# Two groups' weight gradients kept on chip until the last head, and stored in row pieces

## The chip, the cores and the metric

The kernel runs on one core of one Trainium2 chip. The time is what the device takes for one execution, in microseconds, as a median of several runs. A profile of one execution shows the engines (PE for matrix products, DVE, ACT and POOL for the rest, SP for issuing transfers) and the 16 DMA engines that carry every transfer between the device's memory and the chip.

## The reference

The program is the backward pass of one decode step: attention with 32 heads over a cache of 8192 keys and values, beside a gated MLP, both fed by one normalised row. It returns the forward output and the gradients of everything but the MLP's own input.

```python
def _A_ref(x, k_cache, v_cache, wq, wo):          # x: 1 x 1 x 640, caches: 1 x 32 x 8192 x 128
    q = (x @ wq).reshape(B, Sq, Hq, Dh)...
    scores = jnp.einsum("bhqd,bhkd->bhqk", q, k) * (Dh ** -0.5)
    p = _softmax(scores, axis=-1)
    o = jnp.einsum("bhqk,bhkd->bhqd", p, v)
    return o...reshape(B, Sq, Hq * Dh) @ wo

def _B_ref(x, w1, w3, w2):                        # 640 -> 1728 -> 640
    return (silu(x @ w1) * (x @ w3)) @ w2

xn = _layernorm(x)
out = x + _A_ref(xn, ...) + _B_ref(xn, ...)

_out, _vjp = jax.vjp(_f, A_x, A_k_cache, A_v_cache, A_wq, A_wo, B_w1, B_w3, B_w2)
return (out, *_vjp(grad_out))
```

The gradients of the two caches are as large as the caches, 2 MB per head each in bf16. Those of `wq` and `wo` are outer products with one row, 5 MB each in all.

## The kernel before

Head by head, the K and V tiles (128 partitions of 16 KB) are loaded into one of ten slots (`free_slots`, `load_next`), used, overwritten in place with their gradients (`outer`, L474, on DVE) and stored from the same slot (`store`, L485). Loads (L111) and stores (L106) are all issued by SP, in the order in which the program calls them: `store` of a tile is followed by `load_next`, which takes the oldest free slot, and so has to wait until that slot's own store has landed.

Heads come in eight groups of four (`NG`, `GH`), each with a slice of `wq` (`wq_g`, 128 x 5 x 512) and of `wo` (`wo_g`, 128 x 4 x 640), 640 KB each. They live in a pool of three buffers. In the heads after a group has ended, its slices are overwritten with their gradients: `fin_wo` (L521) in the first head of the next group, `fin_wq` (L527), one of five columns `ci` at a time, in the second and third (`side_k`, `side_m`, `side_v`). POOL issues the stores: wo in one transfer (L515), wq a column at a time (L535). After the last column the buffers are free, and POOL loads the slices of the group three ahead (L119, L121); the last such load is that of group 7, after group 4.

The last group's gradients, after head 31, leave in rows: 68 on SP, then 5 and 55 on POOL (`store_group`):

```python
        fifo(dst[0:68], t[0:68])
        for lo, hi in ((68, 73), (73, P)):
            nc.gpsimd.dma_start(dst[lo:hi], t[lo:hi])
```

After the loop over heads come `outers_a` and `outers_b` of head 31 (its V and K gradients and their stores), then `fin_od`, `fin_pe`, `fin_wo` and five times `fin_wq` for group 7, then the two small outputs.

Of the kernel before, what the change touches and what calls it, by code (L numbers as in the profile page):

```python
# [16 lines left out]
P = 128  # L17
# [4 lines left out]
def kernel(  # L22
# [22 lines left out]
    nc = tc.nc  # L45
    H = A_k_cache.shape[1]
# [8 lines left out]
    NG = H // GH  # L55
# [49 lines left out]
    def fifo(out_, in_):  # L105
        nc.sync.dma_start(out_, in_)  # L106
# [10 lines left out]
    def load_group(g, eng):  # L117
        wq_g = wpool.tile([P, NC, GW], BF16, name="wq_g", tag="wq_g")
        eng.dma_start(wq_g[:], wq_v[:, :, g * GW:(g + 1) * GW])  # L119
        wo_g = wpool.tile([P, GH, D], BF16, name="wo_g", tag="wo_g")  # L120
        eng.dma_start(wo_g[:], wo_v[:, g * GH:(g + 1) * GH, :])  # L121
        grp[g] = dict(wq=wq_g, wo=wo_g)
# [175 lines left out]
    hd = {}  # L298
# [180 lines left out]
    def outer_v(h, lo, hi):  # L479
        outer(kv_tiles[("V", h)], hd[h]["qd"][:, 1, :], hd[h]["P2"], lo, hi)  # L480

    def outer_k(h, lo, hi):
        outer(kv_tiles[("K", h)], hd[h]["qd"][:, 0, :], hd[h]["U2"], lo, hi)

    def store(kind, h):  # L485
        t = kv_tiles.pop((kind, h))
        if kind == "K":
            hd.pop(h)
        fifo((dkc if kind == "K" else dvc)[h], t[:])
        free_slots.append(t)  # L490
        load_next()
# [18 lines left out]
        for hh in range(GH):  # L510
            out_row(G_["od_bf"][:, hh, 0:1], G_["wo"][:, hh, :])

    def store_group(g, dst, t):
        if g < NG - 1:
            nc.gpsimd.dma_start(dst, t[:])  # L515
            return
        fifo(dst[0:68], t[0:68])
        for lo, hi in ((68, 73), (73, P)):
            nc.gpsimd.dma_start(dst[lo:hi], t[lo:hi])

    def fin_wo(g):  # L521
        G_ = grp[g]
        for hh in range(GH):
            nc.vector.tensor_scalar(G_["wo"][:, hh, :], g_bc[:], G_["od"][:, hh, 0:1], None, ALU.mult)
        store_group(g, dwo_v[:, g * GH:(g + 1) * GH, :], G_["wo"])

    def fin_wq(g, ci):  # L527
        G_ = grp[g]
        wq_g, dqb = G_["wq"], G_["dqb"]
        nc.vector.scalar_tensor_tensor(wq_g[:, ci, :], wq_g[:, ci, :], 1.0, dqb, ALU.mult, ALU.mult,  # L530
                                       accum_out=dxa[:, ci, g:g + 1])
        nc.vector.tensor_scalar(wq_g[:, ci, :], dqb, xn_col[:, ci:ci + 1], None, ALU.mult)  # L532
        dwq_g = dwq_v[:, :, g * GW:(g + 1) * GW]
        if g < NG - 1:
            nc.gpsimd.dma_start(dwq_g[:, ci, :], wq_g[:, ci, :])  # L535
        if ci == NC - 1:
            if g == NG - 1:
                store_group(g, dwq_g, wq_g)
            grp.pop(g)
            if g + 3 < NG:  # L540
                load_group(g + 3, nc.gpsimd)
# [147 lines left out]
    gate = consts.tile([P, 1], F32, name="gate")  # L689

    def side_k(h):
        g, hh = divmod(h, GH)
        if hh == 1 and g > 0:
            fin_wq(g - 1, 0)
        elif hh == 2 and g > 0:
            fin_wq(g - 1, 3)
        elif hh == 3 and g + 1 < NG:
            prep_do(g + 1, 1)

    def side_m(h):  # L700
        g, hh = divmod(h, GH)
        if hh == 0 and g > 0:
            fin_od(g - 1)
        elif hh == 1 and g > 0:
            fin_wq(g - 1, 1)
        elif hh == 2 and g > 0:
            fin_wq(g - 1, 4)
        elif hh == 3 and g + 1 < NG:
            prep_do(g + 1, 2)
            prep_do(g + 1, 3)  # L710

    def side_v(h):
        g, hh = divmod(h, GH)
        if hh == 0 and g > 0:
            fin_wo(g - 1)
        elif hh == 1 and g > 0:
            fin_wq(g - 1, 2)
        elif hh == 2 and g + 1 < NG:
            prep_new(g + 1)
            prep_do(g + 1, 0)  # L720
        elif hh == 3 and g + 1 < NG:
            prep_cm(g + 1, hd[h]["m"][:, 324:324 + 4 * GH])
# [18 lines left out]
    def outers_a(h):  # L741
        outer_v(h, 0, J // 2)
        outer_v(h, J // 2, J)
        store("V", h)
        outer_k(h, 0, J // 2)

    def outers_b(h):
        outer_k(h, J // 2, J)
        store("K", h)
# [3 lines left out]
    def head(h):  # L753
        nxt = h + 1 < H
        pre = nxt and h + 1 != MLP_AT
        has_prev = h > 0 and h != MLP_AT
        had = (4 if h else 2) if h != MLP_AT else 0
        if nxt:
            new_head(h + 1)
        if has_prev:  # L760
            outers_a(h - 1)
        side_k(h)
        for c in range(had, NCH, 2):
            T(h, "K", c)
            T(h, "K", c + 1)
            if c >= 2:
                Mp(h, "K", c - 2)
            if h > 0 and h % GH == 0 and c == 4:
                col(h - 1)
        T(h, "V", 0)  # L770
        T(h, "V", 1)
        Mp(h, "K", NCH - 2)
        ev(h, "K")
        T(h, "V", 2)
        T(h, "V", 3)
        selm(h, "K")
        mx(h)
        Mp(h, "V", 0)
        T(h, "V", 4)
        mx_bc(h)  # L780
        side_m(h)
        T(h, "V", 5)
        Mp(h, "V", 2)
        expo(h)
        T(h, "V", 6)
        zsum(h)
        probs(h)
        if has_prev:
            outers_b(h - 1)
        side_pe1(h)  # L790
        T(h, "V", 7)
        side_pe1b(h)
        Mp(h, "V", 4)
        side_pe2(h)
        side_v(h)
        if nxt:
            fill_qz(h + 1)
            rows_pe(h + 1, pst()[:, 0:2 * DH], True)
            rows_act(h + 1)
        if pre:  # L800
            T(h + 1, "K", 0)
            T(h + 1, "K", 1)
        Mp(h, "V", NCH - 2)
        ev(h, "V")
        o_sum(h)
        selm(h, "V")
        rdot(h)
        if pre:
            T(h + 1, "K", 2)
        dsum(h)  # L810
        if pre:
            T(h + 1, "K", 3)
            Mp(h + 1, "K", 0)
        dq_sum(h)
        if not nxt:
            col(h)
# [15 lines left out]
    for h in range(H):  # L832
        if h == MLP_AT:
            outers_a(h - 1)
            outers_b(h - 1)
            mlp()
        head(h)
        if h < 2:
            nc.gpsimd.tensor_copy(gate[:], hd[h]["rdot"][:])
            load_group(h + 1, nc.gpsimd)  # L840
    outers_a(H - 1)
    outers_b(H - 1)
    fin_od(NG - 1)
    fin_pe(NG - 1)
    fin_wo(NG - 1)
    for ci in range(NC):
        fin_wq(NG - 1, ci)
# [58 lines left out]
```

## Time and profile before

| what | value |
|---|---|
| median of 3 runs | 730.87 us (730.68 to 731.32) |
| the profiled execution | 730.97 us, of which the span of the profile is 729.2 us |
| busy: PE, DVE, ACT, POOL | 604.1, 459.5, 376.3, 44.0 us |
| bytes moved | 303.53 MB, 416 GB/s over the span |
| queue of SP / of POOL | 277.09 MB / 25.61 MB |

The page gives busy times of the engines, then the span in 40 slices of 18.2 us with the mean busy share of the 16 DMA engines. Further views answer who waited for whom, what ran when, and how busy the engines were in any stretch.

### The profile page before, as it was taken

What the parts mean: (1) busy time and instruction counts of PE and PEld (TensorE: products, weight loads), DVE (VectorE), ACT (ScalarE), POOL (GpSimd) and SP (SyncE); (2) the same over time, 40 slices, a digit from 0 to 9 for tenths busy, and PEclk for the clock granted to TensorE, in tenths of its full rate; (3) what the DMA queues carried; (4) which work ended last, traced back from release to release, by engine and by line L of the source; (5) the groups of instructions that cost most, each with busy time, mean ns of one, the idle gap of its engine ahead of it and who ended that gap; (6) DMA issues with size and microseconds to landing.
All of it is one profiled execution on the core that took longest, in us unless ns stands there. A gap on an engine that the chain in (4) does not pass through costs nothing.

```text
span 729.2 us, 12963 instructions
## 1 busy us (share of the span) xinstructions
PE 604.1 (83%) x5186; PEld 376.4 (52%) x5193; DVE 459.5 (63%) x811; ACT 376.3 (52%) x727; POOL 44.0 (6%) x75
## 2 busy tenths in 40 slices
PE   4989489999899899877886998988898889969930
PEld 2547366665565555544554554554555546545510
DVE  4179646678868776667556665646746657566482
ACT  3640736665665656544554554645554446645510
POOL 0010100010001000101000000000000000000000
PEclk9996799999999999989999998989999989998975
DMA  8999999999999999999999999999999999999994
GB/s 356 394 418 413 432 439 409 418 436 413 422 427 424 425 431 426 428 424 432 420 430 429 431 423 427 426 432 431 422 430 425 433 428 430 431 423 423 429 408 151
DMA packets 24219, 303.53 MB, mean 416 GB/s; under 512 B 3380, under 2 KB 5356, under 8 KB 11487
## 3 DMA queue, kind: packets, MB, share of 16 engines
q1 hardware_dynamic: 17994, 277.09, 89.6%
q0 software_dynamic: 6160, 25.61, 8.8%
q8 instruction: 41, 0.67, 0.4%
q14 instruction: 20, 0.16, 0.1%
q10 hardware_dynamic: 4, 0.00, 0.0%
HBM read 151.34 MB, written 151.34 MB: 415 GB/s over the span
## 4 chain that ended last, share of the span: by engine, by line
DMA 54%; PE 35%; DVE 5%; ACT 2%; issue 1%; SPq 0%; ACTq 0%; DVEq 0%
DMA out_dram<-kv 21%; DMA kv<-in_A_k_cache_dram 18%; PE pT L326 18%; DMA kv<-in_A_v_cache_dram 14%; PE sA L347 5%; PE dA L347 4%; PE X L441 4%; DVE kv L474 3%; PE m L364 2%; DMA wo_g<-in_A_wo_dram 2%; ACT KT L328 1%; PE pT L274 1%; PE m L408 0%; DVE side L265 0%; DVE wq_g L530 0%
## 5 line engine op out<-in xcount | busy, mean ns | idle before, releaser
L328 ACT COPY KT<-pT 128x512 f32<-128x512 f32 x512 | 287.9, 587 | 230.3 <-PE pT L326 210.5
L326 PE MATMUL pT<-ident_f,kv 128*128 128x128 f32 x2048 | 305.9, 288 | 58.6 <-DMA kv<-in_A_k_cache_dram 40.9
L326 PEld LDWEIGHTS pT<-ident_f,kv 128*128 128x128 f32 x2048 | 235.2, 148 | 150.8 <-PE pT L326 53.4
L474 DVE TENSOR_TENSOR kv<-qd,U 128x4096 bf16<-128x4096 bf16 x64 | 146.1, 2285 | 0.0
L474 DVE TENSOR_TENSOR kv<-qd,P 128x4096 bf16<-128x4096 bf16 x64 | 143.6, 2285 | 0.0
L441 PE MATMUL X<-kv,Z 128*32 128x512 bf16 x1024 | 100.3, 424 | 1.8 <-DVE Z L458 1.8
L347 PE MATMUL dA<-KT,qz 128*32 128x512 bf16 x512 | 85.4, 413 | 0.0
L347 PE MATMUL sA<-KT,qz 128*32 128x512 bf16 x512 | 82.6, 402 | 0.0
L424 DVE SCALAR_TENSOR_TENSOR U<-m,P 128x64 bf16<-128x64 f32 x32 | 7.5, 234 | 103.9 <-PE m L364 103.9
L441 PEld LDWEIGHTS <-Z 128*32 128x32 bf16 x1024 | 34.1, 103 | 36.8 <-issue 11.6
L347 PEld LDWEIGHTS <-qz 128*32 128x32 bf16 x1024 | 29.6, 95 | 40.7 <-issue 38.1
L390 DVE TENSOR_REDUCE mrow<-m 128x1 f32<-128x64 f32 x32 | 7.2, 223 | 54.4 <-PE m L364 54.3
L364 PEld LDWEIGHTS m<-selc,KT 64*128 64x128 f32 x256 | 22.2, 148 | 30.4 <-ACT KT L354 17.8
L364 PE MATMUL m<-selc,KT 64*128 64x64 f32 x256 | 31.2, 247 | 7.2 <-ACT KT L354 7.2
L535 POOL DMA_DIRECT2D out_dram<-wq_g x35 | 19.1, 544 | 225.6 <-DVE wq_g L532 130.4
L384 ACT CAST qd<-pT 128x256 bf16<-128x256 f32 x32 | 11.9, 372 | 39.4 <-DVE kv L474 30.4
L397 DVE TENSOR_REDUCE negM<-m 128x1 f32<-128x128 f32 x32 | 9.3, 292 | 33.2 <-PE m L394 33.2
L530 DVE SCALAR_TENSOR_TENSOR wq_g<-wq_g,side 128x512 bf16<-128x512 bf16 x40 | 27.4, 684 | 0.0
L265 DVE SCALAR_TENSOR_TENSOR side<-wo_g,g_bc 128x640 bf16<-128x640 bf16 x32 | 26.3, 820 | 1.1 <-DMA wo_g<-in_A_wo_dram 0.8
L515 POOL DMA_DIRECT2D out_dram<-wo_g x7 | 5.3, 760 | 274.6 <-DVE qz L371 234.5
L456 DVE SCALAR_TENSOR_TENSOR U<-m,P 128x128 bf16<-128x128 f32 x32 | 11.4, 355 | 15.9 <-PE m L454 15.9
L354 ACT COPY KT<-dA 64x512 f32<-64x512 f32 x32 | 18.6, 581 | 4.7 <-PE dA L347 4.6
(163 smaller groups left out, 383.5 us busy)
## 6 DMA issues: line engine op xcount, KB each, us to landing
out_dram<-kv SPq DMA_DIRECT2D x64, 2048.0 KB, 30.8
kv<-in_A_k_cache_dram SPq DMA_DIRECT2D x32, 2048.0 KB, 15.4
kv<-in_A_v_cache_dram SPq DMA_DIRECT2D x32, 2048.0 KB
wq_g<-in_A_wq_dram POOLq DMA_DIRECT2D x7, 640.0 KB, 15.1
wo_g<-in_A_wo_dram POOLq DMA_DIRECT2D x7, 640.0 KB, 22.1
out_dram<-wo_g POOLq DMA_DIRECT2D x7, 640.0 KB, 13.5
out_dram<-wq_g POOLq DMA_DIRECT2D x35, 128.0 KB, 8.2
kv<-in_B_w_dram SPq DMA_DIRECT2D x2, 1728.0 KB
```

What stands on the lines that cost most here:

```text
L265: nc.vector.scalar_tensor_tensor(junk[:], G_["wo"][:, hh, :], 1.0, g_bc[:], ALU.mult, ALU.mult, accum_out=G_["do"][:, hh:hh + 1])
L326: nc.tensor.transpose(pT[:, k * P:(k + 1) * P], W3[:, 4 * c + k, :], ident_f[:])
L328: nc.scalar.copy(KT[:].rearrange("p k w -> p (k w)"), pT[:])
L347: nc.tensor.matmul(S_[kind][q:q + QW, :], lhsT=S_["qz"][:, o:o + QW], rhs=KTb[c][:, par, :], start=(c0 == 0 and par == 0), stop=(c0 == NCH ...
L354: nc.scalar.copy(XS[0:QH].rearrange("p k w -> p (k w)"), S_.pop(kind)[0:QH, :])
L364: nc.tensor.matmul(S_["m"][:, b0:b0 + 4 * J].rearrange("p (x c k t) -> p k x c t", x=4, k=4, t=2)[:, k], lhsT=XS[0:QH, k, :], rhs=selc[0:Q ...
L384: nc.scalar.copy(qd[:].rearrange("p a d -> p (a d)"), hd[h].pop("ps_r"))
L441: nc.tensor.matmul(xg["X"][q:q + QW, :], lhsT=Z[:, o:o + QW], rhs=W[:, N4 * i:N4 * (i + 1)], start=(slot == 0 and i < 4), stop=(slot == NS ...
L456: nc.vector.scalar_tensor_tensor(S_["U2"][:], S_["V"][:, 0:J].unsqueeze(2).to_broadcast([P, J, 2]), S_["m"][:, OC + NS:OC + NS + 1], S_["P ...
L474: nc.vector.tensor_tensor(dst[:, lo * DH:hi * DH].rearrange("p (j a b) -> p j a b", a=DH // 2, b=2), vec.rearrange("p (a b) -> p a b", b=2 ...
L530: nc.vector.scalar_tensor_tensor(wq_g[:, ci, :], wq_g[:, ci, :], 1.0, dqb, ALU.mult, ALU.mult, accum_out=dxa[:, ci, g:g + 1])
L535: nc.gpsimd.dma_start(dwq_g[:, ci, :], wq_g[:, ci, :])
```

## The change

Groups 5 and 6 (`HOLD`) no longer store their gradients when they are ready: `store_group` notes destination and tile in `held`. Four such tiles are collected, wo and wq of group 5, then wo and wq of group 6. wq of these groups also gives up its five columns and is stored whole.

After the loop over heads, before head 31's outer products, POOL copies a value of head 31 (`rdot`) to a scratch tile, so that it waits for it, and `flush(2)` twice sends wo and wq of group 5: 5 and 121 rows on POOL and 2 rows on SP. When wo of group 7 has been sent as before, `flush(68)` sends wo of group 6 as 68 rows on SP and 5 and 55 on POOL, and `flush(2)` its wq as 5, 121 and 2 rows. wq of group 7 is last. On SP the two 2-row pieces of group 5 stand between the store of head 30's K gradient and that of head 31's V gradient.

```diff
+    HOLD = (NG - 3, NG - 2)
+    held = []
+
+    def store_group(g, dst, t, late=(68, 5)):
+        if g in HOLD:
+            held.append((dst, t))
+            return
         if g < NG - 1:
             nc.gpsimd.dma_start(dst, t[:])
             return
-        fifo(dst[0:68], t[0:68])
-        for lo, hi in ((68, 73), (73, P)):
-            nc.gpsimd.dma_start(dst[lo:hi], t[lo:hi])
+        store_rows(dst, t, *late)
+
+    def store_rows(dst, t, n, k):
+        if n < P // 2:
+            cuts = ((0, k), (k, P - n), (P - n, P))
+            hw = 2
+        else:
+            cuts = ((0, n), (n, n + k), (n + k, P))
+            hw = 0
+        for i, (lo, hi) in enumerate(cuts):
+            (nc.sync if i == hw else nc.gpsimd).dma_start(dst[lo:hi], t[lo:hi])
...
         store_group(g, dwo_v[:, g * GH:(g + 1) * GH, :], G_["wo"])
+        if g == NG - 1:
+            flush(68)
+            flush(2)
+
+    def flush(n):
+        dst, t = held.pop(0)
+        store_rows(dst, t, n, 5)
...
-        if g < NG - 1:
+        if g < NG - 3:
             nc.gpsimd.dma_start(dwq_g[:, ci, :], wq_g[:, ci, :])
         if ci == NC - 1:
-            if g == NG - 1:
+            if g >= NG - 3:
                 store_group(g, dwq_g, wq_g)
...
+    nc.gpsimd.tensor_copy(gate[:], hd[H - 1]["rdot"][:])
+    flush(2)
+    flush(2)
     outers_a(H - 1)
     outers_b(H - 1)
     fin_od(NG - 1)
```

More of the change, by code (lines that the diff above doesn't have):

```diff
@@ L511, in fin_pe @@
             out_row(G_["od_bf"][:, hh, 0:1], G_["wo"][:, hh, :])
-    def store_group(g, dst, t):
+    HOLD = (NG - 3, NG - 2)
[4 more added lines that the diff above has]
+            return
         if g < NG - 1:
```

## The prediction, made before the changed kernel was run

> **What bounds the kernel now.** I read the 40 slices of the page first, then SP's waits, then the end of the timeline, then a table of the last 40 us.
>
> ```profile
> DMA  8999999999999999999999999999999999999994
> GB/s 356 394 418 413 432 439 409 418 436 413 422 427 424 425 431 426 428 424 432 420 430 429 431 423 427 426 432 431 422 430 425 433 428 430 431 423 423 429 408 151
> DMA packets 24219, 303.53 MB, mean 416 GB/s; under 512 B 3380, under 2 KB 5356, under 8 KB 11487
> ...
> SPq L111 <- DMA out_dram<-kv: 472.5, 52, 22.4
> SPq L106 <- DVE kv L474: 86.8, 14, 10.5
> ```
>
> The DMA engines are full from the second slice to the last but one. SP, which issues the cache loads (L111), spends 472.5 us in waits until an older cache store has landed and its slot is free. A store has landed when all 16 DMA engines have done their share, so the slowest of them sets the pace. The end shows it:
>
> ```profile
> core 0: us, PE busy (x) PEld busy (x) DVE busy (x) ACT busy (x) POOL busy (x), PEclk, DMA share, GB/s
> ...
> 700.00:705.00 5.00, 0.00 (x0) 0.00 (x0) 5.00 (x3) 0.00 (x0) 0.00 (x0) 0.62 0.95 400
> ...
> 713.00:716.00 3.00, 0.82 (x3) 0.58 (x3) 1.71 (x11) 0.00 (x0) 1.32 (x2) 0.50 0.83 316
> ...
> 718.00:720.00 2.00, 0.00 (x0) 0.00 (x0) 0.00 (x0) 0.00 (x0) 0.00 (x0) 0.50 0.49 147
> ...
> 722.00:724.00 2.00, 0.00 (x0) 0.00 (x0) 0.00 (x0) 0.00 (x0) 0.00 (x0) 0.50 0.08 33
> 724.00:726.00 2.00, 0.00 (x0) 0.00 (x0) 0.00 (x0) 0.00 (x0) 0.00 (x0) 0.50 0.06 25
> ```
>
> The last compute ends at 716.4 us. From 722 on the DMA share is 0.06 to 0.08, one engine in sixteen, at 25 GB/s. The packet records agree: 16,384-byte packets follow one another every 0.607 us until 727.6, all of one engine, the second half of head 31's V gradient and the whole of its K gradient. Its last arrival is at 728.0, and 1.2 us later the span ends (729.2). I call it the late engine. The arrivals of its last four cache transfers are 711.8, 717.0, 723.1 and 728.0; the second-latest engine has the last three at 708.6, 713.6 and 720.2, and the leaders finish K31 at 712.3. So the end is the late engine's total work, and it never starves: it takes up V31's store near 716.5, issued at 701, and K31's at 722.7, issued at 705.5.
>
> ```profile
> 601.00:644.00 43.00, 38.48 (x342) 24.04 (x342) 31.16 (x46) 25.38 (x51) 0.76 (x1) 1.00 1.00 429
> 644.00:687.00 43.00, 36.67 (x294) 22.36 (x294) 25.10 (x44) 21.59 (x43) 2.70 (x5) 0.88 1.01 426
> ...
> PE pT L326 <- DMA kv<-in_A_k_cache_dram: 11.0, 4, 3.9
> PE pT L326 <- DMA kv<-in_A_v_cache_dram: 4.9, 4, 2.1
> ```
>
> The last two rows are PE's waits from 560 to 700 us: 15.9 us in which compute waits for loads. Faster loads would be used.
>
> **The change, part by part.** No byte is added.
>
> *Removed between 552 and 680 us:* the stores of wo and wq of groups 5 and 6, 640 KB each.
>
> ```profile
> 633.71 0.76 POOL L515 DMA_DIRECT2D out_dram<-wo_g  x1 [44.60 <-DVE qz L371]
> ...
> 645.30 0.54 POOL L535 DMA_DIRECT2D out_dram<-wq_g  x1 [10.83 <-DVE wq_g L532]
> ...
> 672.07 0.54 POOL L535 DMA_DIRECT2D out_dram<-wq_g  x1 [1.90 <-DVE wq_g L532]
> ...
> 708.37 1.31 POOL L519 DMA_DIRECT2D out_dram<-wo_g  x2 [35.76 <-DVE wo_g L524]
> ...
> 708.10 0.32 SPq L106 DMA_DIRECT2D out_dram<-wo_g  x1
> ...
> 713.09 0.26 SPq L106 DMA_DIRECT2D out_dram<-wq_g  x1
> ```
>
> Each is spread over all 16 engines, 8 rows of 5 KB on each. A wo share is 8 packets of 5,120 bytes at 0.196 us, 1.57 us; a wq share is 10 packets of 4,096 bytes at 0.157 us, 1.57 us. Four stores take 6.28 us off every engine. On the late engine that is 6.28 us off the end, all but 0.6 us of it (two of five wq columns of group 6, issued at 669.6 and 672.1) ahead of the load of K31, so head 31's compute shifts by up to 5.7 us too. PE's 15.9 us of load waits cover that; without that cover the late engine would still have its queue, since V31's store has 15 us in hand and K31's 17.
>
> *Added at the end:* the same 2.56 MB in row pieces. How rows go to engines is read from group 7, which already leaves as 68, 5 and 55 rows. Its wq rows on POOL make 71 packets of 4,096 and 16 of 1,024 bytes: one remainder on each of 16 engines, which fits 5 engines with one row and 11 with five (6 x 4,096 + 1,024). The late engine shows one row of it (4,096 + 1,024), then six 16-byte dummies for the 55-row piece. The 68 rows arrive on four engines (717.1 to 717.9 for wo). So 121 rows should go as 11 rows on the same 11 engines, and the 2 rows to two of the four. [...] The late engine thus takes back 4 rows, 4 x 0.196 = 0.8 us, and some 50 dummies at 0.009 us, 0.45 us.
>
> *Crowding.* Row pieces slow the others' packets. Until 710 us hardly a 16 KB packet exceeds 0.611 us; between 712 and 720, with group 7's pieces under way, the late engine has two of 1.14 and 1.11 us. Its step from 717.0 to 723.1 is 6.1 us where eight packets need 4.86; less its own row and dummies some 1.0 us is left, and 0.1 in the step before. So two held-back gradients cost it 1.1 us. Four more: 2.3 us at the same price; at least 0 (the pieces of 5 and 121 rows are mostly not the 68-row kind that ran beside it); at most 5.2, if each of the 140 KB that others now read holds up the late engine for the 0.037 us per KB it would have needed itself. I take 2.3, the measured row.
>
> *Issue costs.* POOL gets the gate copy, behind head 31's dot product (DVE L424, 695.4), then four pieces at about 0.66 us, 2.6 us, free long before wo of group 7 at 708.4 (POOL is idle for 35.8 us there). At 708.4 wo7, wo6 and wq6 take 6 x 0.66 = 4 us and end before wq7 is due at 713.4. Uncovered they cost that much on wq7's pieces, not on the late engine. SP issues two 2-row pieces, 0.6 us, between K30's store (695.2) and V31's (701.0), where it waits on DVE; wo6 and wq6 add 0.6 us before 713.1, where it waits 4.7 us on DVE (L851). No load follows into the held buffers (the last, of group 7, uses group 4's), so holding them blocks nobody. All this is nothing.
>
> *Sum for the late engine:* 728.0 - 6.28 + 0.8 + 0.45 + 2.3 = 725.3, that is -2.7 us. Of the profiled execution's 730.97 us 1.77 lie outside the span; the median shown, 730.87, is 0.1 below it. Forecast 730.87 - 2.7 = 728.2.
>
> **The others at the end.** The four engines with 68 rows land wq7 by 722.4. They gain 17 rows of wo6 (68 packets of 1,280 bytes at 0.052 us, 3.5 us) and up to seven single rows, 1.4 us, and are 5.7 us earlier: 721.6. The eleven take 3 x 11 + 5 = 38 more rows, 7.45 us; the worst of them lands wq7 at 721.3 now, then 721.3 - 5.7 + 7.45 = 723.1. So the late engine still ends last, by 2.2 us.
>
> **Rivals.**
> - *No crowding* (0.22): the two slow packets came from the 68-row wq piece alone. Then the eleven decide, 723.1 to 723.5, and the time is 730.87 - 4.7 = 726.2. For: wo's step shows only 0.1 us. Against: 4,096-byte packets are up to 0.5 us late between 716 and 718, too.
> - *The rows still pass the late engine's door* (0.13): crowding at its upper end, 5.2 us. 728.0 - 6.28 + 1.25 + 5.2 = 728.2, no change, 731.0. [...] Against it: group 7's 70 KB in others' hands would have cost 2.6 us, and 1.1 were seen.
> - *The eleven become the bound, slower* (0.10): between 712 and 720 POOL's row packets took 1.3 (5,120 bytes) to 1.5 (4,096) times their quiet duration. With a stretch f the worst of the eleven ends at 715.6 + 7.45 f: it passes the late engine's 725.3 at f = 1.3, the old end at 1.67 and 729.5, measurably slower, at 1.87. At f = 2 it is 730.5, the time 733.4. For: eleven engines then read scattered rows at once. Against: durations overlap, so throughput suffers less.
> - *121 rows spread evenly* (0.05): the late engine keeps three of four shares, 4.7 us; gain 0.7 at most, 730.3.
>
> **Numbers.** Forecast case 0.50 (727 to 729.3), the rest as given. A change under 0.2% (1.5 us) is no change for this measurement. Faster: 0.50 + 0.22 = 0.72; same: 0.13 + 0.05 = 0.18; slower: 0.10. The range reaches from the no-crowding case, 725.8 with 0.4 for its spread, to the middle of the no-change case, 731.0; outside lie the slower case, the upper half of the no-change case and a little below.
>
> **What would show it.** Right: gradient stores of groups 5 and 6 gone from POOL's timeline between 552 and 680; K31's load landing 5 to 6 us earlier; DMA share above 0.9 until some 718 and a one-engine end under 2 us. Wrong: the one-engine end still 5 us long (crowding or an even spread), or several engines busy after 726 (the eleven bound).

## The result and the profile after

The changed kernel takes 736.45 us (735.92 to 737.03), the kernel before, run beside it, 730.45 us: a ratio of 1.0082, 95% interval 1.0069 to 1.0095. It is 6.0 us slower where 2.7 us faster was forecast; the range ended at 731.0.

The slices of the page, of the profiled execution with a span of 734.9 us, show the end first.

```profile
DMA  9999999999999999999999999999999999999994
GB/s 350 394 417 416 439 432 403 424 430 422 414 432 426 425 426 428 428 429 425 429 426 429 429 428 426 430 425 430 427 429 425 431 433 425 428 432 425 391 340 125
```

The share stays at its top until the last slice, but the bytes do not follow: 391 and 340 GB/s in the two slices before the last, where the kernel before had 429 and 408 in the same places. The engines are busy with packets that take longer: 16 KB takes up to 1.9 us after 712, against a median of 0.611 over the run. The table by stretches (its last two columns are DMA share and GB/s) places it:

```profile
644.00:687.00 43.00, 38.07 (x312) 23.24 (x311) 26.72 (x45) 23.88 (x48) 0.00 (x0) 0.92 1.00 428
687.00:700.00 13.00, 5.13 (x56) 2.92 (x56) 11.59 (x11) 1.40 (x5) 3.27 (x5) 0.75 0.94 368
...
710.00:715.00 5.00, 0.06 (x1) 0.00 (x0) 0.28 (x1) 0.00 (x0) 0.00 (x0) 0.50 0.98 286
715.00:720.00 5.00, 0.00 (x0) 0.00 (x0) 0.00 (x0) 0.00 (x0) 0.00 (x0) 0.50 0.89 245
...
726.00:728.00 2.00, 0.00 (x0) 0.00 (x0) 0.00 (x0) 0.00 (x0) 0.00 (x0) 0.50 0.23 80
728.00:730.00 2.00, 0.00 (x0) 0.00 (x0) 0.00 (x0) 0.00 (x0) 0.00 (x0) 0.50 0.05 19
730.00:732.00 2.00, 0.00 (x0) 0.00 (x0) 0.00 (x0) 0.00 (x0) 0.00 (x0) 0.50 0.06 25
```

From 710 to 720 us the DMA engines are 0.9 to 1.0 busy at 245 to 286 GB/s, against 428 in the middle of the run. And the one-engine end is still there, from 728 on. The arrival records of the last five cache transfers on the late engine tell when it lost its time:

| kernel | fifth last | fourth | third (K30) | V31 | K31 |
|---|---|---|---|---|---|
| before | 706.8 | 711.8 | 717.0 | 723.1 | 728.0 |
| after | 700.8 | 706.8 | 715.2 | 727.0 | 732.3 |

At 700.8 it is 6.0 us ahead, close to the 6.28 of the sum. Then two transfers that took 5.2 and 6.1 us take 8.4 and 11.8. Its 16 KB packets of 0.611 us take 0.8 to 1.9 us between 717.9 and 726.6; after that, with the others done, most are back at 0.611.

The timeline of POOL and SP has a second, smaller thing:

```profile
705.88 1.03 POOL L533 DMA_DIRECT2D out_dram<-wq_g  x1 [0.86 <-DMA out_dram<-wo_g]
707.89 0.57 POOL L533 DMA_DIRECT2D out_dram<-wq_g  x1 [0.98 <-DVE junk L885]
722.23 0.76 POOL L533 DMA_DIRECT2D out_dram<-wq_g  x1 [13.77 <-DMA out_dram<-wq_g]
...
718.62 4.30 SPq L881 DMA_DIRECT2D out_dram<-KT  x2
727.06 5.52 SPq L899 DMA_DIRECT2D out_dram<-fin_bf  x2
```

In this trace four of the last transfers go out only when the one eight places before them on their queue has landed. POOL now has twelve pieces: the tenth waits 0.9 us for the second (landed 705.6), and the twelfth, the 55 rows of wq of group 7, is ready at 707.9 and waits 13.8 us for the fourth, the 121 rows of wq of group 5 (landed 721.9). SP has four more transfers: the first half of the last output (L899) is issued at 727.1, when V31's store has landed (727.0), and the second at 732.3, with K31's; before the change they were issued at 717. The second lands at 733.4. POOL's pieces, too, reach the late engine's end behind K31: the last of them lands its last share at 733.3. Before the change the last output and the last piece had landed at 722.5 and 726.2, ahead of K31. From K31's last arrival to the end it is now 2.6 us, not 1.2.

### The profile page after: what moved, and what is told of

It is laid out like the page before. It is cut to its first block, busy times and chain, and to the rows that moved or that the text cites. A ratio compares the mean times of both kernels' runs of the same rounds, so it can differ in the third digit from the quotient of the medians.

```text
span 734.9 us, 12963 instructions
## 1 busy us (share of the span) xinstructions
PE 603.3 (82%) x5186; PEld 375.8 (51%) x5193; DVE 459.9 (63%) x811; ACT 376.5 (51%) x727; POOL 43.1 (6%) x72
## 4 chain that ended last, share of the span: by engine, by line
DMA 50%; PE 36%; DVE 6%; issue 3%; ACT 2%; SPq 0%; POOLq 0%; POOL 0%; ACTq 0%; DVEq 0%
DMA kv<-in_A_k_cache_dram 25%; DMA out_dram<-kv 17%; PE pT L326 17%; DMA kv<-in_A_v_cache_dram 6%; PE sA L347 5%; PE X L441 4%; PE dA L347 4%; DVE kv L474 3%; PE m L364 2%; DMA wo_g<-in_A_wo_dram 2%; ACT KT L328 1%; PE gu_ps L590 1%; PE dh_ps L601 1%; PE acc L207 1%; PE m L468 1%
## 5 line engine op out<-in xcount | busy, mean ns | idle before, releaser
L556 POOL DMA_DIRECT2D out_dram<-wq_g x25 | 13.7, 547 | 158.2 <-DVE wq_g L553 110.2
L414 DVE RECIPROCAL rZ<-m 128x1 f32<-128x1 f32 x32 | 5.3, 167 | 24.2 <-PE m L408 24.2
```

## The experiments

All are the changed kernel with one edit, unless it says otherwise. The kernel before, run beside them, had medians of 730.96, 731.06 and 731.03 us in the three sets.

**Nothing stored.** What is the removal worth alone?

```diff
     def flush(n):
-        dst, t = held.pop(0)
-        store_rows(dst, t, n, 5)
+        held.pop(0)
```

> As the changed kernel, but the four held tiles are not stored at all. All theories: the late engine is rid of 6.28 us and the crowding is that of before, 730.5 - 6.3 = 724.2. If it is above 727, the saving in the middle, and not the crowding at the end, was mis-sized.

Measured: 724.65 us, ratio 0.991 (0.9894 to 0.9927). The late engine lands K31 at 722.2, 5.8 us before the kernel before. The saving was sized almost rightly (6.28); most of the miss lies in what comes back at the end, 732.3 - 722.2 = 10.1 us on the late engine, where 3.55 were expected (0.8 + 0.45 + 2.3). Another 0.5 us is missing from the saving itself, and 1.4 us come behind K31's arrival. Arrivals come from one execution of each kernel. Near 555 us, where the kernels compared have done the same work, the arrivals of one store lie between 554.6 and 555.9 us, so differences of arrivals hold to about 1 us.

**Whole tiles.** The same bytes at the same places, but each tile in one transfer, as the kernel before stores it: 8 rows to an engine by the prediction's count.

```diff
-        store_rows(dst, t, n, 5)
+        nc.gpsimd.dma_start(dst, t[:])
```

> As the changed kernel, but the four held tiles leave whole (128 rows, one transfer each on POOL) at the places where their row pieces left. Theory D (door): the late engine is slowed because other DMA engines read partitions that lie behind its own door to the chip's memory, so a tile sent whole, where each engine reads only its own partitions, crowds nobody: the late engine gets its 6.28 us back and the end is that of before, 730.5 +- 1. Rival T (traffic): any gradient traffic with small rows beside the last cache stores slows them, whoever reads it: the late engine has 6.28 us more than in the changed kernel besides the crowding, 738 to 742. Rival L (lateness): what costs is only that the 2.56 MB come last; then whole or in pieces they end alike, 736 or more.

Measured: 732.96 us, ratio 1.0027 (1.0016 to 1.0037), 2.0 us above before and 3.5 below the changed kernel. That misses all three ranges, Theory D's by 1.5 us and the others' by 3 to 5. K31 lands at 729.5, 7.3 us after the kernel that stores nothing: 6.28 of its own rows and 1.0 more. POOL's last piece lands behind it, at 730.4, and the end is 2.3 us after K31's arrival instead of 1.2. Traffic or lateness alone, then, costs the late engine 1 us, not 10.

**Lower or upper partitions.** The same number of rows and pieces, from one half or the other.

```diff
-        store_rows(dst, t, n, 5)
+        for eng, lo, hi in ((nc.gpsimd, 0, 5), (nc.gpsimd, 5, 60), (nc.sync, 60, 64)):
+            eng.dma_start(dst[lo:hi], t[lo:hi])     # upper half: 64, 69, 124, 128
```

> As the changed kernel, but of each held tile only partitions 0 to 63 are stored (5 and 55 rows on POOL, 4 on SP); the rows 64 to 127 are left out. Theory D: the late engine's eight partitions lie in one half; if in this one, the crowding is nearly whole, 733 to 736; if not, none is left and the late engine keeps its saving of 5 us, 725.5. Rivals T and L: half the traffic in either half, half the crowding of 10 us: 730 to 731, and alike in both halves.

> As the kernel with the low half, but the partitions 64 to 127 are stored (5, 55 and 4 rows) and the rows 0 to 63 left out; the bytes and pieces are the same. Theory D: the opposite of the low half, 725.5 against 733 to 736, whichever way round. Rivals T and L: the same as the low half, 730 to 731.

Measured: lower half 735.85 us (1.0066, 1.0051 to 1.0081), upper half 728.61 (0.9968, 0.9956 to 0.998). Half the bytes out of the lower partitions cost nearly all that the change costs; the same bytes out of the upper ones leave most of the saving. K31 lands at 730.9 and at 724.2. That is 8.7 and 2.0 us after the kernel that stores nothing, 6.7 apart. Of the three theories only that of the door tells the halves apart. The upper half's median is 3 us above the 725.5 expected, of which the late engine has 0.75; most of the rest comes behind K31's arrival: POOL's last piece lands at 725.8 and SP's last output at 725.3, and the end is 3.1 us after K31 instead of 1.2.

**Eight rows.** Which partitions? Rows 16 to 19 and 48 to 51 alone, against 20 to 23 and 52 to 55. That the first eight are the late engine's was the author's guess.

```diff
-        store_rows(dst, t, n, 5)
+        for lo in (16, 48):                         # the other kernel: (20, 52)
+            nc.sync.dma_start(dst[lo:lo + 4], t[lo:lo + 4])
```

> As the changed kernel, but of each held tile only eight rows are stored, 16 to 19 and 48 to 51, in two 4-row transfers on SP (one row on each of the four engines that carry the 68 rows); the other 120 rows are left out. Theory D (door), narrowed: the late engine is the one that gets one row of each group-7 gradient and none of the 68, by count the fifth, and its own partitions are these eight. Then all 160 KB pass its door: 724.65 (nothing stored) + 2.5 to 10, that is 727 to 734. If its partitions are others, or if it is not a matter of partitions, 725 and the same as the next kernel.

> [...] Theory D: the late engine is not touched, 724.5 to 725.5. Rivals: as the kernel before it.

Measured: 732.48 us and 726.61 us, 1.0022 (1.0013 to 1.0032) and 0.994 (0.9925 to 0.9955) of before. Two stretches of the first, rows 16 and 48 on, from its table by stretches:

```profile
722.00:724.00 2.00, 0.00 (x0) 0.00 (x0) 0.00 (x0) 0.00 (x0) 0.00 (x0) 0.50 0.31 83
...
726.00:728.00 2.00, 0.00 (x0) 0.00 (x0) 0.00 (x0) 0.00 (x0) 0.00 (x0) 0.50 0.11 41
```

The same two of the second, rows 20 and 52 on:

```profile
722.00:724.00 2.00, 0.00 (x0) 0.00 (x0) 0.00 (x0) 0.00 (x0) 0.00 (x0) 0.50 0.04 13
...
726.00:728.00 2.00, 0.00 (x0) 0.00 (x0) 0.00 (x0) 0.00 (x0) 0.00 (x0) 0.50 0.00 0
```

With the first eight rows, about 0.31 of the engines, five of sixteen, are busy at 722 us and move 83 GB/s, where five engines at the late engine's own pace of 16 KB in 0.607 us would move 135: they are slower than that. The late engine's packets say so, too: from 712.9 to 725.8 eleven of 16 KB follow one another at 1.0 to 1.2 us each. With the neighbours' eight rows the stretch from 722 is nearly empty. The late engine lands K31 at 728.0 and 722.1; with nothing stored it was 722.2. So 32 rows, 160 KB, out of exactly these partitions delay it by 5.8 us, and the neighbouring rows delay it by nothing. The late engine's door stands here for these eight partitions alone; why reads of them by others delay it, no run shows. The two kernels' rows also go to other addresses in the device's memory, and no run varies that alone.

The 5.8 us are 0.036 us per KB, close to what the late engine would have taken to read these rows itself (0.607 us for 16 KB, 6.1 us for all). But this is an average of two unequal halves:

| kernel | V29 | K30 | V31 | K31 |
|---|---|---|---|---|
| rows 16 and 48 on | 695.3 | 711.3 | 720.3 | 728.0 |
| rows 20 and 52 on | 695.9 | 710.9 | 716.1 | 722.1 |

The 80 KB of group 5 are read between V29 and K30 (they have landed by 701.3): the first kernel, 0.6 us ahead, falls 0.4 behind, so they cost 1.0 us. Another 5.5 us come after K30 with the 80 KB of group 6, beside the pieces of group 7. Why the first half was cheap was not tried.

The second kernel's 2.0 us over the one that stores nothing are not the late engine's: SP, with eight more transfers, issues the last output at 722.4 instead of 713.

**In the middle, not at the end.** The pieces leave when the tiles are ready.

```diff
-            held.append((dst, t))
+            for lo, hi in ((0, 5), (5, 126)):
+                nc.gpsimd.dma_start(dst[lo:hi], t[lo:hi])
             return
...
     def flush(n):
-        dst, t = held.pop(0)
-        store_rows(dst, t, n, 5)
+        pass
```

> Nothing is held: the tiles of groups 5 and 6 leave as soon as they are ready, but in POOL's pieces of 5 and 121 rows; the last two rows are left out. Theory D: the rows cross the late engine's door in the middle of the run as well, and as it has no idle time there, the crowding of some 9 us costs as much: 731 to 735. Rival E (end): the crowding comes of many pieces falling together at the end; in the middle the late engine just loses its 6.28 us: 725 to 727.

Measured: 730.24 us, ratio 0.9985 (0.9975 to 0.9995), between both expectations. The last three of the sixteen arrivals show who lost:

| kernel | V29's store | K31's store |
|---|---|---|
| before | 692.6, 692.8, 701.9 | 718.6, 720.2, 728.0 |
| nothing stored | 687.5, 687.7, 696.2 | 712.2, 712.4, 722.2 |
| pieces at once | 696.4, 696.5, 696.8 | 725.2, 725.7, 726.0 |

At V29's store, when the pieces have landed (687.1), the last arrival is only 0.6 us behind the kernel that stores nothing, or 1.8 counting that it was 1.2 ahead near 555; own rows and dummies are 1.25 by the prediction's count. So the late engine keeps most of its saving. The next engines are 8.8 us behind that kernel and level with the last. At K31 the last arrival is 2.0 us earlier than before the change, the two ahead of it 5.5 to 6.6 us later, and the run ends on neither: the 68 rows of wq of group 7 land at 728.0, the last output at 728.2. So in the middle the pieces hold up the other engines far more than the late one. Theory D did not say that, and it is not the free saving of Rival E. Why the others lose their time was not tried.

**The same with all rows, and for group 6 alone.**

```diff
-            held.append((dst, t))
+            store_rows(dst, t, 2, 5)
             return
...
-    HOLD = (NG - 3, NG - 2)
+    HOLD = (NG - 2,)                                # the second kernel alone
...                                                   # flush does nothing in both; in the second
                                                      # fin_wq tests NG - 2 in place of NG - 3
```

> The tiles of groups 5 and 6 leave as soon as they are ready, as 5 and 121 rows on POOL and 2 on SP: all rows, nothing held. Theory D: as without the two last rows, about 0.8 us below before, 730.2 +- 0.7, with the late engine some 2 us earlier than before and the others later. Rival E, that crowding comes only of the end, gives 725 to 727.

> The same for group 6 alone: wo and wq of group 6 in pieces of 5, 121 and 2 rows when ready, group 5 as before the change. Theory D: half of the change of the full dose, 730.6 +- 0.7. If crowding grows faster than the dose, the half dose is the best of all, 729.

Measured: 730.29 us (0.999, 0.9978 to 1.0002) and 730.97 us (0.9998, 0.999 to 1.0007). Both agree with the time of the first expectation and neither is told from the kernel before. In the profiled execution of the second, K31 lands at 725.4, 2.6 us earlier than before, but the 68 rows of wq of group 7 land at 727.0 and the last output at 727.1, so most of that gain does not reach the end. No dose is better than another by what can be measured here, and no version that stores all rows beats the kernel before.

**A small dose at the end.** Only wo of group 6 is held and leaves as 68, 5 and 55 rows.

```diff
-        if g in HOLD:
+        if g == NG - 2 and not wq:
...
             flush(68)
-            flush(2)
...
-        if g < NG - 3:
+        if g < NG - 1:
...
-    nc.gpsimd.tensor_copy(gate[:], hd[H - 1]["rdot"][:])
-    flush(2)
-    flush(2)
```

> Only wo of group 6 is held and leaves as 68, 5 and 55 rows after wo of group 7; everything else as before the change. The late engine saves 1.57 us and takes one row back (0.2). Theory D with the price seen for group 7's own pieces (0.4 us per us of door time): -0.8 us, 730.1. With the price seen in the changed kernel (1.7): +0.8, 731.8. Rival E: -1.3, 729.6.

Measured: 732.36 us (730.72 to 734.1), ratio 1.0021 (1.0012 to 1.0031), 1.3 us slower, beyond both prices of the door theory. The profiled execution, the fastest of its ten, lands K31 at 727.0, 1.0 us earlier than before, while its runs scatter over 3.4 us. It does not settle the price; it shows that one tile brings no gain either.

**Group 7 whole.** The kernel before, without its own row pieces.

```diff
-        fifo(dst[0:68], t[0:68])
-        for lo, hi in ((68, 73), (73, P)):
-            nc.gpsimd.dma_start(dst[lo:hi], t[lo:hi])
+        nc.gpsimd.dma_start(dst, t[:])
```

> The kernel before, but the two gradients of group 7 leave whole instead of in 68, 5 and 55 rows. The late engine reads 16 rows more than now (14 net of its two single rows, 2.7 us) and the other engines keep out of its door. Theory D with door rows at full price (16 rows or 80 KB, 2.9 us): no change, 731 +- 0.7. With the price of the prediction (1.1 us of crowding for both tiles): 732.6. With the price of the changed kernel (2.3 us a tile): 729.

Measured: 732.49 us, ratio 1.0024 (1.0012 to 1.0035): near the price of the prediction, 1.1 us for these two tiles, if whole tiles hold up nobody (four of them cost the late engine 1.0 us above). From 711.8 (711.7) the late engine needs 17.8 us for its last three transfers instead of 16.2.

## Why the prediction was wrong, point by point

- *What bounds the kernel*: right. One late DMA engine ends the run, and its arrivals move with its work: 6.28 us forecast off it, 5.8 measured with nothing put back.
- *The engines of the pieces*: right in number. On POOL the two 121-row pieces of wq end in 22 packets of 3,072 bytes, one on each of eleven engines for each tile, as 11 rows (13 x 4,096 + 3,072) would.
- *Crowding, 2.3 us with an upper bound of 5.2*: the step that failed. With the late engine's own rows and dummies (1.25 in the sum) it came to 10.1 us. The upper-half kernel measures own rows, dummies and pieces out of the upper half at 2.0 where 1.25 were counted. The rows at the late engine's door are 5.8 of the 10.1 by the eight-row kernels, and 6.7 by the difference of the two halves: the case that had 0.13. Its price of 5.2 came near, but at an even 0.037 us per KB; the eight-row kernel has 1.0 us for its first 80 KB and 5.5 for the rest, so that the sum fits is partly luck. Some 1.4 to 2.3 us are left over when door rows and other rows come together at the end; no run took them apart. In the middle of the run the late engine loses little (0.6 to 1.8 us at V29's store), and the other engines lose more (8.8 us the next ones).
- *Where the 2.3 came from*: group 7's pieces do cost near 1.1 us; the whole-tile kernel bears that row out. The error was to carry it to other pieces in other company. What decides the price is open: the same eight rows of a tile, read by the same kind of transfer, were cheap for group 5 and dear for group 6, beside group 7's pieces.
- *Against the rival* it was held that 70 KB in group 7 would have cost 2.6 us and cost 1.1. One small sample of a shared resource was used as a price for twice that load on top of it; as a bound it should have been the full time of all rows at the end, group 7's too, and more.
- *Issue costs at nothing*: the end, 1.4 us further behind K31's arrival, was not in the sum. It counted POOL's and SP's instructions, but not the waits for the transfer eight places before (13.8 us on POOL), nor POOL's pieces that are still to be worked off on the late engine when K31 is through. SP's wait puts the last output behind K31's store (733.4); POOL's last piece lands at 733.3, with two of the late engine's own rows done after K31. Either would have put the end about there. POOL's 13.8 us of wait hit other engines, which have these 55 rows by 728.2.
- *Compute*: right, PE's load waits covered the shift, and head 31's dot product ended some 6 us earlier (POOL's gate copy at 689.4, against 695.4).

The span's 5.7 us are so accounted: -5.8 saved, +10.1 at the end on the late engine, +1.4 behind it.

## What to carry to other kernels

Giving a slow DMA engine's rows to others need not relieve it: here 160 KB out of eight partitions, read by other engines, delayed it by 5.8 us, and as much out of the neighbouring eight not at all. Ask which partitions the rows come from, not only whose queue they leave. Bound contention by the full time of the shared resource before taking a cheap sample of it as the price: 80 KB cost 1.0 us at one time and as many, beside others, 5.5 at another. When one engine is relieved, look at the next ones: here the pieces sent at once brought them level with it (696.4, 696.5 and 696.8 at V29's store). When transfers are cut into pieces, count them, and see which late one would wait: here POOL's twelfth waited 13.8 us for its fourth.

## What the runs showed that was not expected

- Rows 16 to 19 and 48 to 51, read by other engines, delay the late DMA engine (K31 at 728.0, with nothing stored 722.2); rows 20 to 23 and 52 to 55 do not (722.1). Before the change it lands each of the last three cache transfers 7.8 to 9.5 us after the second-latest. Why it is late was not tried.
- A piece of few rows is not free for the engines that carry none of it: in the POOL queue they show 16-byte packets in its place, 77 for group 7's four pieces and 331 for the twelve of the changed kernel, in turn with the 16 KB packets of the cache stores.
- The delay by rows 16 to 19 and 48 to 51 is 5.8 us for 160 KB, 0.036 us per KB on average, but 1.0 us for the first half of it.
